# Transposing attention probabilities for tiles 4 to 23: one VectorE block transpose and eight SBUF-to-SBUF DMAs

## The chip, the core and the metric

The program runs on one core of a Trainium2 chip. The metric is the device time of one execution in microseconds (us), smaller is better. TensorE is called PE here, VectorE DVE, ScalarE ACT; SP is the queue from which this kernel issues all its DMAs. A "burst" is the run of small matmuls that PE does for one attention step.

## What is computed

A chunked local attention over 4 x 8 heads and 768 positions, followed by two feed-forward layers over all 3072 tokens:

```
scores = scale * q_chunk @ k_full.T          # chunk of 32, 16 left, 8 right, 8 memory keys
a = exp(scores - max); a = a / (sum(a) + 1e-9)
out_chunk = a @ v_full
x = out transposed to [3072, 512]
g = relu(x @ w_in) + alpha * min(x @ w_in, 0);  x = g @ w_out
h = x @ w2_in;  out = (h * tanh(softplus(h))) @ w2_out
```

## The kernel before

The 3072 tokens are worked in six blocks of 512 (four attention tiles of 128 tokens each, so 24 tiles T = 0 to 23). Layer 0 (first feed-forward) goes over the six blocks, then layer 1 does. In each block, `gemm1` (L697) makes 16 hidden groups j of 128 features, and `gemm2` (L761) adds them up; each is 12 matmuls of 128x512, since every fp32 product is made of three products of a high and a low half (`wh`,`wl` and `xh`,`xl` or `gh`,`gl`). The weights of layer 0 arrive in a raw form during block 0, and for each of the 32 weight tiles ACT does a scaling (L313) and a cast (L332) and DVE four instructions (L316, L319, L322, L335). The last of them, L335, writes the low half; `gemm2` of group j needs it by its third matmul.

Attention tiles 0 to 3 come first. Tiles 4 to 23 are woven into the layer-0 matmuls one block ahead: the burst "sv" does the scores of tile T+1 (L473) and right behind them the values of tile T (L540). Between the scores and the values of one tile lie: the maximum (DVE L488), eight exponentials (ACT L491), the normalisation (DVE L507) and the transposition of the probabilities `s` into `aT`, which puts keys on partitions. That last step is done in two ways:

- T < 7, `turn_pe`: PE transposes (16 small ones per tile, L583), then two copies from PSUM (L591, on ACT for tiles 4 to 6).
- T >= 7, `turn_dve`: eight DVE block transposes of 32 partitions x 256 (L609), each of which also moves its rows to other partitions.

For T >= 4 there is one `s` buffer and one `aT` buffer. Every step is entered in a `Plan` with an engine and an estimated duration; the planner (`run`, L107) works out an order for each engine, by what is due first among what it believes ready, and the program is issued in that order. Every engine, and SP's queue, then works strictly in its order. `block_steps` (L653 on) says which attention steps a block holds, `weave` spreads them evenly over the positions of the block. The engine's tile layer gives each DMA one of eight completion semaphores in turn, so a DMA waits until the eighth one before it has landed.

Of the kernel before, what the change touches and what calls it, by code (L numbers as in the profile page):

```python
# [68 lines left out]
class Plan:  # L69
# [13 lines left out]
    def add(self, eng, dur, fn, reads=(), writes=(), at=None, not_before=0.0):  # L83
        i = len(self.tasks)
        deps = set()
        for bufs, w in ((reads, False), (writes, True)):
            for b in bufs:
                b, part = (b[0], b[1:]) if isinstance(b, tuple) else (b, ())
                deps.update(t for t, p, tw in b.uses if (w or tw) and all(x == y for x, y in zip(p, part)))
                if w:  # L90
                    self.replaced.extend((i, old) for old in b.after)
                b.uses.append((i, part, w))
        deps.discard(i)
        if eng == "pe":
            at = self.now
            self.now += dur
        self.tasks.append((eng, dur, fn, deps, at, not_before))
        return i
# [76 lines left out]
def chunked_attention_moe_moe_kernel(  # L175
# [16 lines left out]
    nc = tc.nc  # L192
    P = 128
    B, UPB, W, H, D = vw.shape
# [5 lines left out]
    NP = H // 2  # L200
# [6 lines left out]
    CH = 32  # L207
    SW = 16 + CH + 8 + NM
# [1 line left out]
    TB = BN // P  # L210
    BLOCKS = [(t0, BN) for t0 in range(0, NT, BN)]
    NBA = len(BLOCKS)
    UPT = 7
    BOTH = ("act", "dve")
    WHOLE = (3,)
    T0 = BLOCKS[0][1] // P
# [20 lines left out]
    add = plan.add  # L237


    def a_(n):  # L240
        return 0.1 + 0.83e-3 * n

    def d_(n, fast=False):
        return 0.066 + n / (1920.0 if fast else 960.0)
# [4 lines left out]
    def copy_on(eng, out, in_):  # L249
        (nc.scalar.copy if eng == "act" else nc.vector.tensor_copy)(out, in_)  # L250
# [125 lines left out]
    def wide_of(b):  # L376
        return b.t.rearrange("p (g w) -> p g w", w=P)
# [20 lines left out]
    def att_bank(T, late):  # L398
        n_ps[0] += 1
        return bank((0, 1, 2, 4, 5, 6, 7)[n_ps[0] % 7] if T < T0 else late)  # L400
# [50 lines left out]
    def scores_of(T):  # L451

        t = T % TPB
        (kt, kview), (qt, qview) = kts[T], qs[T]
        bk = att_bank(T, 6)
        sb = s_bufs[T % 2 if T < T0 else 0]

        def s():
            return wide_of(sb)[:, :, CH : CH + SW]

        st = stats.next()
        ss[T] = sb

        def ps():
            return bk.t.rearrange("p (g c) -> p g c", c=SW)


        def go():
            for e in range(2):
                for p in range(NP):  # L470
                    for c in range(2):
                        k0 = e * (U + NM) + c * CH
                        nc.tensor.matmul(  # L473
                            ps()[c * 64 : (c + 1) * 64, e * NP + p, :],
                            qview()[:, p, e].rearrange("p h (x c) -> p (h x) c", c=2)[:, :, c],
                            kview()[:, p, k0 : k0 + SW],
                            start=True, stop=True,
                        )


        def clip():
            if t == 0:
                nc.vector.memset(ps()[0:64, 0:NP, 0:16], NEG)
            if t == TPB - 1:
                nc.vector.memset(ps()[64:128, NP:, SW - 8 :], NEG)

        def top():
            nc.vector.tensor_reduce(st.t[:, 0, :], ps(), AX.X, ALU.max, negate=True)  # L488

        def exps(g):  # L490
            nc.scalar.activation(  # L491
                s()[:, g, :], ps()[:, g, :], AF.Exp, bias=st.t[:, 0, g : g + 1], scale=0.125,
                accum_out=st.t[:, 1, g : g + 1],
            )


        def less():
            nc.vector.tensor_add(s(), ps(), st.t[:, 0, :].unsqueeze(2).broadcast_to([P, 2 * NP, SW]))

        def exp():  # L500
            nc.scalar.activation(s(), s(), AF.Exp, scale=0.125)

        def total():
            nc.vector.tensor_reduce(st.t[:, 1, :], s(), AX.X, ALU.add)

        def norm():
            nc.vector.tensor_mul(s(), s(), st.t[:, 2, :].unsqueeze(2).broadcast_to([P, 2 * NP, SW]))  # L507

        def rest():
            if t in (0, TPB - 1):  # L510
                add("dve", 0.15, clip, [], [bk])
            add("dve", d_(512), top, [bk], [(st, 0)])
            if T in WHOLE:
                add("dve", d_(512), less, [(st, 0), bk], [sb])
                add("act", a_(512), exp, [], [sb])
                add("dve", d_(512), total, [sb], [(st, 1)])
            else:
                add("dve", 0.12, lambda: nc.vector.tensor_scalar_mul(st.t[:, 0, :], st.t[:, 0, :], 0.125), [], [(st, 0)])
                for g in range(2 * NP):
                    add("act", 0.29, lambda g=g: exps(g), [(st, 0), bk], [(sb, g), (st, 1, g)])  # L520
            add("dve", 0.12, lambda: nc.vector.tensor_scalar_add(st.t[:, 2, :], st.t[:, 1, :], 1e-9), [(st, 1)], [(st, 2)])
            add("dve", 0.14, lambda: nc.vector.reciprocal(st.t[:, 2, :], st.t[:, 2, :]), [], [(st, 2)])
            add("dve", d_(512), norm, [(st, 2)], [sb])
            att_bufs.append(st)

        return go, [kt, qt], [bk], rest
# [41 lines left out]
    def turn_pe(T):  # L568
        sb = ss.pop(T)
        ab = a_bufs[T % 2 if T < T0 else 0]  # L570

        def aT():
            return ab.t[:W].rearrange("k (g h c q) -> k g h c q", g=2 * NP, h=2, c=2)

        aTs[T] = ab, aT
        for c in range(2):
            bk = att_bank(T, 6 + c)

            def turn(bk=bk, c=c):
                rows = slice(c * 64, (c + 1) * 64)  # L580
                k0 = (1 - c) * CH
                for g in range(2 * NP):
                    nc.tensor.transpose(  # L583
                        bk.t[0:W, g * 64 : (g + 1) * 64], wide_of(sb)[rows, g, k0 : k0 + W], ident[rows, rows]
                    )

            def back(eng, bk=bk, c=c):
                copy_on(eng, aT()[:, :, :, c, :], bk.t[0:W].rearrange("k (g h q) -> k g h q", g=2 * NP, h=2))

            add("pe", 0.6, turn, [sb] + behind(T), [bk])  # L590
            add(BOTH if T < T0 else "act", a_(512), back if T < T0 else partial(back, "act"), [bk], [(ab, c)])  # L591

    def turn_dve(T):

        sb, ab = ss.pop(T), a_bufs[0]

        def aT():
            return ab.t.rearrange("k (g h c q) -> k g h c q", g=2 * NP, h=2, c=2)

        aTs[T] = ab, aT  # L600
        for c in range(2):
            for h in range(2):
                for b in range(SW // CH):

                    def turn(c=c, h=h, b=b):
                        rows = slice((2 * c + h) * CH, (2 * c + h + 1) * CH)
                        keys = slice((c + b) * CH, (c + b + 1) * CH)
                        cols = slice(CH + b * CH, CH + (b + 1) * CH)
                        nc.vector.transpose(aT()[keys, :, h, c, :], wide_of(sb)[rows, :, cols])  # L609

                    add("dve", 0.34, turn, [sb], [(ab, (c, h, b))])

    def new_x(n):
        x = xring.next()
# [2 lines left out]
    def behind(T):  # L617

        return [last[0]] if T >= T0 and last else []
# [12 lines left out]
    def run_step(st):  # L632
        kind, T = st
        if kind == "t":
            turn_pe(T)
        elif kind == "v":
            burst(T, values_of(T))
        elif kind == "s":
            burst(T, scores_of(T))
        else:  # L640

            burst(T, scores_of(T), values_of(T - 1))
        if kind in ("s", "sv") and T0 - 1 <= T < NTT - 1:
            load_qk(T + 1)
        if kind in ("v", "sv"):
            done = T if kind == "v" else T - 1
            if T0 - 1 <= done < NTT - 1:
                load_v(done + 1)
        if kind in ("s", "sv") and T >= UPT:
            turn_dve(T)  # L650

    first = "s0 s1 t0 s2 t1 s3 v0 t2 v1 t3 v2 v3"
    block_steps = [[(st[0], int(st[1:])) for st in first.split()]]  # L653
    block_steps.append([("s", T0)])
    for T in range(T0, 2 * T0):
        block_steps[1] += [("t", T)] * (T < UPT) + [("sv", T + 1)]
    for blk in range(2, NBA):
        block_steps.append([("sv", T + 1) if T + 1 < NTT else ("v", T) for T in range(blk * TB, (blk + 1) * TB)])

# [172 lines left out]
    for st in block_steps[0]:  # L832
        run_step(st)
# [16 lines left out]
    for layer, blk, j in tiles:  # L850
# [13 lines left out]
        h = early[j] if (layer, blk) == (0, 0) and j < SPLIT else gemm1(layer, blk, j, xcur, n)  # L864
# [78 lines left out]
```

## Time and profile before

| what | value |
|---|---|
| time, median of 3 runs | 1127.35 us (1127.08 to 1128.28) |
| profiled execution: its own time / span | 1127.35 us / 1125.6 us |
| granted PE clock | 0.999 of full |
| busy PE / DVE / ACT | 1118.5 us (99%) / 828.1 us (74%) / 583.6 us (52%) |
| chain that ended last | PE 88%, DVE 8%, issue 1% |
| L609, DVE block transposes | 136 of 435 ns, 59.1 us |
| L583, PE transposes | 112 in all, 48 of them for tiles 4 to 6 |

The span begins with the first instruction of the profile and ends with the last; the time of the run has 1.75 us more around it. Matmul ends are modelled, so that PE is shown busy also where a matmul waited in its pipeline; the start times of successive matmuls tell the pace.

### The profile page before, as it was taken

Reading aid. Unit: us, or ns where it says so; the run is one execution under the profiler, and the core shown is the slowest. Engines: PE = TensorE matmul, PEld = TensorE weight load, DVE = VectorE, ACT = ScalarE, POOL = GpSimd, SP = SyncE. Lnnn points to the kernel's source line nnn. Section 1 sums busy time; section 2 is a strip of 40 time slices with the busy share of each in tenths; the row PEclk is TensorE's granted clock in tenths of the full one; section 3 lists DMA queues with packets and bytes.
Section 4 is the critical chain, followed back from the end, with each engine's and each line's share of the span. In section 5 each row is a group of like instructions: output and inputs, shape, how many; then the busy total and the mean of one; then the engine's idle time right before and its main releaser. Section 6 shows DMA issues by size and latency. Waiting matters only on the chain.

```text
span 1125.6 us, 16616 instructions
## 1 busy us (share of the span) xinstructions
PE 1118.5 (99%) x6320; PEld 921.7 (82%) x6320; DVE 828.1 (74%) x1452; ACT 583.6 (52%) x1270; POOL 6.8 (1%) x20
## 2 busy tenths in 40 slices
PE   9999999999999999999999999999999999999998
PEld 6888888888888888888888888888888888888886
DVE  7999954576667658645548778778878778777775
ACT  6887544454445545445446445446446445444543
POOL 2000000000000000000000000000000000000000
PEclk9999999999999999999999999999999999999999
DMA  9876312264454544434333002002001000100101
GB/s 279 240 224 186 90 44 53 70 190 120 120 158 121 155 137 134 124 103 132 102 94 103 1 1 75 1 1 75 1 1 63 13 1 20 38 1 1 38 1 38
DMA packets 71456, 94.28 MB, mean 84 GB/s; under 512 B 25296, under 2 KB 41680, under 8 KB 71376
## 3 DMA queue, kind: packets, MB, share of 16 engines
q1 hardware_dynamic: 71376, 93.22, 28.1%
q8 instruction: 49, 0.80, 0.3%
q14 instruction: 31, 0.25, 0.1%
HBM read 72.23 MB, written 20.97 MB: 83 GB/s over the span
## 4 chain that ended last, share of the span: by engine, by line
PE 88%; DVE 8%; issue 1%; ACT 0%; DVEq 0%
PE bank L761 43%; PE bank L697 42%; DVE wf L319 2%; DVE wf L322 1%; PE bank L473 1%; PE bank L540 1%; DVE gl L710 1%; DVE wf L316 1%; DVE rstrip L719 1%; DVE wo L335 1%; DVE aT L609 1%; DVE wi L335 0%; DVE s L507 0%; DVE st L488 0%; DVE xl L561 0%
## 5 line engine op out<-in xcount | busy, mean ns | idle before, releaser
L697 PE MATMUL bank<-xh,wi 128*128 128x512 f32 (+1 forms) x1552 | 506.2, 388 | 0.0
L697 PEld LDWEIGHTS bank<-xh,wi 128*128 128x128 f32 x1552 | 290.5, 188 | 60.1
L697 PE MATMUL bank<-xl,wi 128*128 128x512 f32 (+1 forms) x776 | 300.2, 387 | 0.0
L761 PE MATMUL bank<-gh,wo 128*128 128x512 f32 x768 | 254.0, 391 | 0.0
L761 PE MATMUL bank<-wo,gh 128*128 128x512 f32 x768 | 236.4, 389 | 0.0
L697 PEld LDWEIGHTS bank<-xl,wi 128*128 128x128 f32 x776 | 145.7, 188 | 29.2
L761 PEld LDWEIGHTS bank<-gh,wo 128*128 128x128 f32 x768 | 144.0, 188 | 30.9 <-DVE wo L335 0.4
L761 PEld LDWEIGHTS bank<-wo,gh 128*128 128x128 f32 x768 | 144.1, 188 | 29.9
L761 PE MATMUL bank<-gl,wo 128*128 128x512 f32 x384 | 149.5, 389 | 0.0
L761 PE MATMUL bank<-wo,gl 128*128 128x512 f32 x384 | 149.4, 389 | 0.0
L709 ACT CAST gh<-u 128x512 fp32r<-128x512 f32 x96 | 59.9, 623 | 155.9 <-PE bank L761 155.7
L719 DVE SCALAR_TENSOR_TENSOR rstrip<-rstrip,nalpha 128x512 f32<-128x512 f32 x96 | 71.9, 749 | 78.3 <-ACT rstrip L716 77.9
L709 ACT CAST gh<-rstrip 128x512 fp32r<-128x512 f32 x96 | 59.8, 623 | 108.5 <-PE bank L761 62.2
L710 DVE TENSOR_TENSOR gl<-rstrip,gh 128x512 fp32r<-128x512 f32 x96 | 66.1, 689 | 59.0 <-ACT gh L709 57.7
L715 ACT ACTIVATE rstrip<-bank 128x512 f32<-128x512 f32 x96 | 57.6, 600 | 97.4 <-PE bank L697 94.3
L728 ACT ACTIVATE u<-bank 128x512 f32<-128x512 f32 x96 | 57.4, 598 | 93.5 <-PE bank L697 92.7
L733 DVE SCALAR_TENSOR_TENSOR e<-n,rc 128x512 f32<-128x512 f32 x96 | 66.4, 691 | 48.5 <-ACT rc L732 48.5
L710 DVE TENSOR_TENSOR gl<-u,gh 128x512 fp32r<-128x512 f32 x96 | 66.3, 690 | 42.5 <-ACT gh L709 42.5
L761 PEld LDWEIGHTS bank<-wo,gl 128*128 128x128 f32 x384 | 72.1, 188 | 14.9
L761 PEld LDWEIGHTS bank<-gl,wo 128*128 128x128 f32 x384 | 72.1, 188 | 14.7
L731 ACT ACTIVATE e<-n,two 128x512 f32<-128x512 f32 x96 | 69.2, 720 | 4.4 <-DVE n L730 4.4
L734 DVE SCALAR_TENSOR_TENSOR rc<-e,rc 128x512 f32<-128x512 f32 x96 | 66.4, 691 | 3.2
(88 smaller groups left out, 1042.6 us busy)
## 6 DMA issues: line engine op xcount, KB each, us to landing
wi<-in_w_in_dram SPq DMA_DIRECT2D x16, 512.0 KB, 9.5
wo<-in_w_out_dram SPq DMA_DIRECT2D x16, 512.0 KB, 9.8
raw<-in_w_in_dram SPq DMA_DIRECT2D x16, 512.0 KB, 4.3
raw<-in_w_out_dram SPq DMA_DIRECT2D x16, 512.0 KB, 4.5
vw<-in_vw_dram SPq DMA_DIRECT2D x21, 384.0 KB, 3.9
kt<-in_kw_dram SPq DMA_DIRECT2D x21, 336.0 KB, 5.0
yd<-rstrip SPq DMA_DIRECT2D x24, 256.0 KB, 2.5
raw<-yd SPq DMA_DIRECT2D x24, 256.0 KB, 2.8
```

Source lines behind the costliest of these rows:

```text
L316: nc.vector.tensor_scalar(f.t, words()[1], 3, 0x7FFFFFFF, ALU.logical_shift_left, ALU.bitwise_and)
L319: nc.vector.scalar_tensor_tensor(f.t, words()[1], 0x80000000, f.t, ALU.bitwise_and, ALU.bitwise_or)
L697: nc.tensor.matmul(bk.t[:, lo:hi], a, b, start=kk == 0 and i == 0, stop=kk == KT - 1 and i == 2)
L709: add("act", a_(n), lambda: nc.scalar.copy(g.t[0], src.t[0]), [src], [(g, "h")])
L710: add("dve", d_(n), lambda: nc.vector.tensor_sub(g.t[1], src.t[0], g.t[0].bitcast(F32)), [src, (g, "h")], [(g, "l")])
L715: add("act", a_(n) - 0.05, lambda: nc.scalar.activation(m.t[0], h.t[:, :n], AF.Relu, scale=-1.0), [h], [m])
L719: lambda: nc.vector.scalar_tensor_tensor(r.t[0], m.t[0], nalpha[:, j : j + 1], r.t[0], ALU.mult, ALU.add),
L728: add("act", a_(BN) - 0.05, lambda: nc.scalar.activation(u.t, hs(), AF.Exp), [h], [u])
L731: add("act", a_(BN) + 0.09, lambda: nc.scalar.activation(e.t, n.t, AF.Ln, bias=two[:, 0:1]), [n], [e])
L733: add("dve", d_(BN), lambda: v.scalar_tensor_tensor(e.t, n.t, 2.0, r.t, ALU.add, ALU.mult), [n, r], [e])
L734: add("dve", d_(BN), lambda: v.scalar_tensor_tensor(r.t, e.t, 2.0, r.t, ALU.subtract, ALU.mult), [e], [r])
L761: nc.tensor.matmul(bk.t[:, :n], lt, rh, start=j == 0 and i == 0, stop=j == NJ - 1 and i == 2)
```

## The change

Tiles 4 to 23 are all transposed by a new function, `turn_dma`. The normalised probabilities of these tiles lie densely in the first 512 columns of `s`. One DVE instruction transposes all 32x32 blocks of all 128 partitions into columns 512 to 1023 of the same buffer, and eight DMAs on SP's queue, of 32 partitions x 256 columns (32 KB) each, carry the blocks to the partitions where `aT` wants them. `aT` is laid out anew (h, c, g, q in place of g, h, c, q), for the first four tiles too. The steps "t" of tiles 4 to 6 are gone, so block 0 holds five attention steps in place of eight and `weave` spaces them differently. `turn_pe` is left for tiles 0 to 3, with 0.85 in place of 0.6 as its estimate.

```
-    UPT = 7
...
-            return wide_of(sb)[:, :, CH : CH + SW]
+            return wide_of(sb)[:, :, CH : CH + SW] if T < T0 else sb.t[:, :512].rearrange("p (g w) -> p g w", w=SW)
...
-            return ab.t[:W].rearrange("k (g h c q) -> k g h c q", g=2 * NP, h=2, c=2)
+            return ab.t[:W].rearrange("k (h c g q) -> k g h c q", g=2 * NP, h=2, c=2)
...
-            add("pe", 0.6, turn, [sb] + behind(T), [bk])
+            add("pe", 0.85, turn, [sb] + behind(T), [bk])
...
-    def turn_dve(T):
+    def turn_dma(T):
...
+        def blocks():
+            nc.vector.transpose(
+                sb.t[:, 512:].rearrange("p (b g q) -> p b g q", b=SW // CH, q=CH),
+                sb.t[:, :512].rearrange("p (g b k) -> p b g k", b=SW // CH, k=CH),
+            )
+
+        add("dve", 0.85, blocks, [], [sb])
         for c in range(2):
-            for h in range(2):
-                for b in range(SW // CH):
-
-                    def turn(c=c, h=h, b=b):
-                        rows = slice((2 * c + h) * CH, (2 * c + h + 1) * CH)
-                        keys = slice((c + b) * CH, (c + b + 1) * CH)
-                        cols = slice(CH + b * CH, CH + (b + 1) * CH)
-                        nc.vector.transpose(aT()[keys, :, h, c, :], wide_of(sb)[rows, :, cols])
-
-                    add("dve", 0.34, turn, [sb], [(ab, (c, h, b))])
+            for b in range(SW // CH):
+
+                for h in range(2):
+
+                    def move(c=c, b=b, h=h):
+                        x0 = (2 * h + c) * 256
+                        nc.sync.dma_start(
+                            ab.t[(c + b) * CH : (c + b + 1) * CH, x0 : x0 + 256],
+                            sb.t[(2 * c + h) * CH : (2 * c + h + 1) * CH, 512 + b * 256 : 512 + (b + 1) * 256],
+                        )
+
+                    add("sp", 0.15, move, [sb], [(ab, (c, h, b))])
...
-        if kind in ("s", "sv") and T >= UPT:
-            turn_dve(T)
+        if kind in ("s", "sv") and T >= T0:
+            turn_dma(T)
...
-        block_steps[1] += [("t", T)] * (T < UPT) + [("sv", T + 1)]
+        block_steps[1] += [("sv", T + 1)]
```

What this does to the order of the instructions is shown at three places, all in block 0.

DVE, around the transposition of tile 8, the last one of block 0, before (`wo` and `wf` are weights of layer 0 and their scratch tile, `st` the statistics of the softmax):

```order
L322 SCALAR_TENSOR_TENSOR wf_1553<-wo_1328,wf_1553 128x512
L319 SCALAR_TENSOR_TENSOR wf_1568<-wo_1394,wf_1568 128x512
L521 TENSOR_SCALAR st_1536<-st_1536 128x8
L322 SCALAR_TENSOR_TENSOR wf_1568<-wo_1394,wf_1568 128x512
L522 RECIPROCAL st_1536<-st_1536 128x8
L335 TENSOR_TENSOR wo_1582<-wf_1553,wo_1582 128x512
L507 TENSOR_TENSOR s<-s,st_1536 128x8x64
L719 SCALAR_TENSOR_TENSOR rstrip<-rstrip,nalpha 128x512
L609 STREAM_TRANSPOSE aT<-s 32x8x32 x8
```

and the same place of the changed kernel (lines there are one lower up to about L650, and ten higher from L707 on):

```order
L520 TENSOR_SCALAR st_1490<-st_1490 128x8
L321 SCALAR_TENSOR_TENSOR wf_1523<-wo_1337,wf_1523 128x512
L521 RECIPROCAL st_1490<-st_1490 128x8
L720 TENSOR_TENSOR gl<-rstrip,gh 128x512
L506 TENSOR_TENSOR s<-s,st_1490 128x512
L334 TENSOR_TENSOR wo_1548<-wf_1523,wo_1548 128x512
L603 STREAM_TRANSPOSE s<-s 128x512
L321 SCALAR_TENSOR_TENSOR wf_1520<-wo_1386,wf_1520 128x512
L729 SCALAR_TENSOR_TENSOR rstrip<-rstrip,nalpha 128x512
```

Eight instructions have become one, and the third instruction on the last weight tile (L322, now L321) and the last L719 stand behind the transposition in place of ahead of it.

SP, the end of block 0's loads, before:

```order
L299 DMA wo_1328<-in_w_out_dram 128x1024
L447 DMA vw_1343<-in_vw_dram 96x2x512
L413 DMA kt_1359<-in_kw_dram 128x672
L433 DMA qbd_101<-in_q_dram 64x8x64 x2
L299 DMA wo_1394<-in_w_out_dram 128x1024
```

and now:

```order
L298 DMA wo_1337<-in_w_out_dram 128x1024
L616 DMA aT<-s 32x256 x8
L432 DMA qbd_101<-in_q_dram 64x8x64 x2
L298 DMA wo_1386<-in_w_out_dram 128x1024
L446 DMA vw_1434<-in_vw_dram 96x2x512
L412 DMA kt_1445<-in_kw_dram 128x672
L432 DMA qbd_90<-in_q_dram 64x8x64 x2
L616 DMA aT<-s 32x256 x8
```

The two groups of eight are the moves of tiles 7 and 8; the load of the last weight tile of layer 0 (`wo15`) stands behind those of tile 7.

PE, where tile 4 was transposed before:

```order
L697 MATMUL bank_692<-xl_359,wi_662 128x512
L697 MATMUL bank_692<-xh_358,wi_662 128x512
L583 MATMUL bank_720<-ident,s 96x64 x8
L583 MATMUL bank_732<-ident,s 96x64 x8
L761 MATMUL bank_604<-gh,wo_696 128x512
```

and the burst that now uses tile 4's `aT`:

```order
L707 MATMUL bank_811<-xh_357,wi_802 128x512
L472 MATMUL bank_819<-kt_667,qbd_101 64x64 x16
L539 MATMUL bank_836<-aT,vw_635 64x64 x16
L707 MATMUL bank_811<-xh_357,wi_802 128x512
L707 MATMUL bank_811<-xl_358,wi_802 128x512
```

The rows of L583 are gone for tiles 4 to 6. The values of tiles 4 to 8 now stand behind 123, 180, 246, 300 and 384 large matmuls of block 0 and its successor, before behind 120, 192, 264, 309 and 384; from tile 8 on the places are the same as before.

## Rows read from the trace of the kernel before

**Rows 1.** Windows view (us): busy time (count) per engine, clock, DMA share, GB/s

```profile
110.00:120.00 10.00, 10.00 (x50) 7.98 (x47) 10.00 (x19) 5.74 (x12) 0.00 (x0) 1.00 0.43 100
```

**Rows 2.** Chain of waits in order of time: start, length, what

```profile
130.20 2.96 PE bank L697 x12
...
1107.67 13.61 PE bank L761 x60
```

**Rows 3.** PE timeline around tile 4's transposition: start, length, line

```profile
46.74 0.39 PE L697 MATMUL bank<-xh,wi 128*128 128x512 f32 x1
47.05 0.92 PE L583 MATMUL bank<-ident,s 64*96 64x64 f32 x16
...
48.24 0.40 PE L761 MATMUL bank<-gl,wo 128*128 128x512 f32 x1
```

**Rows 4.** PE timeline: weight tile wo13, and the bursts of tiles 8 and 9

```profile
119.69 0.73 PE L761 MATMUL bank<-gh,wo 128*128 128x512 f32 x2
...
127.64 1.18 PE L473 MATMUL bank<-kt,qbd 128*64 128x64 f32 x32
128.65 1.55 PE L540 MATMUL bank<-aT,vw 96*64 96x64 f32 x32
130.13 0.50 PE L697 MATMUL bank<-xh,wi 128*128 128x512 f32 x1
...
147.72 1.10 PE L540 MATMUL bank<-aT,vw 96*64 96x64 f32 x32
148.75 0.50 PE L697 MATMUL bank<-xh,wi 128*128 128x512 f32 x1
```

**Rows 5.** DVE timeline of the end of block 0

```profile
105.11 3.59 DVE L609 STREAM_TRANSPOSE aT<-s 32x256 f32<-32x256 f32 x8
108.73 0.43 DVE L316 TENSOR_SCALAR wf<-wo 128x512 uint32<-128x512 uint32 x1
...
118.95 0.68 DVE L335 TENSOR_TENSOR wo<-wf,wo 128x512 fp32r<-128x512 f32 x1
119.55 0.16 DVE L518 TENSOR_SCALAR st<-st 128x8 f32<-128x8 f32 x1
...
121.21 0.42 DVE L316 TENSOR_SCALAR wf<-wo 128x512 uint32<-128x512 uint32 x1
...
124.75 0.74 DVE L719 SCALAR_TENSOR_TENSOR rstrip<-rstrip,nalpha 128x512 f32<-128x512 f32 x1
125.41 3.59 DVE L609 STREAM_TRANSPOSE aT<-s 32x256 f32<-32x256 f32 x8
```

**Rows 6.** Groups by line: count, busy us, mean ns, idle before

```profile
L609 DVE STREAM_TRANSPOSE aT<-s 32x256 f32<-32x256 f32 x136 | 59.1, 435 | 2.6
L322 DVE SCALAR_TENSOR_TENSOR wf<-wi,wf 128x512 uint32<-128x512 uint32 x16 | 10.9, 682 | 0.1
L521 DVE TENSOR_SCALAR st<-st 128x8 f32<-128x8 f32 x24 | 4.0, 168 | 7.0 <-ACT s L491 6.8
```

**Rows 7.** SP timeline: start and length of the issue of DMAs

```profile
148.86 0.33 SPq L447 DMA_DIRECT2D vw<-in_vw_dram  x1
149.25 0.44 SPq L413 DMA_DIRECT2D kt<-in_kw_dram  x1
```

**Rows 8.** Time from issue to landing: stores L784; DMA view, loads of q

```profile
DMA to landing us min/median/max: 2.0/2.1/2.6
...
qbd<-in_q_dram SPq DMA_DIRECT2D x40, 128.0 KB, 5.5
```

**Rows 9.** Line L540 from 146 to 150 us, and PE's weight loads there

```profile
L540 PEldq EVENT_SEMAPHORE  x1: 51/51/51, 147.1 to 147.1; - x1
...
147.66 1.02 PEld L540 LDWEIGHTS bank<-aT,vw 96*64 96x64 f32 x32
```

**Rows 10.** DVE timeline, tile 9: normalisation and last transposes

```profile
136.46 0.69 DVE L507 TENSOR_TENSOR s<-s,st 128x512 f32<-128x512 f32 x1
...
139.71 2.26 DVE L609 STREAM_TRANSPOSE aT<-s 32x256 f32<-32x256 f32 x5
```

More of the change, by code (lines that the diff above doesn't have):

```diff
@@ L588, in back @@
                 copy_on(eng, aT()[:, :, :, c, :], bk.t[0:W].rearrange("k (g h q) -> k g h q", g=2 * NP, h=2))
-            add("pe", 0.6, turn, [sb] + behind(T), [bk])
+            add("pe", 0.85, turn, [sb] + behind(T), [bk])
             add(BOTH if T < T0 else "act", a_(512), back if T < T0 else partial(back, "act"), [bk], [(ab, c)])
-    def turn_dve(T):
+    def turn_dma(T):
         sb, ab = ss.pop(T), a_bufs[0]
         def aT():
-            return ab.t.rearrange("k (g h c q) -> k g h c q", g=2 * NP, h=2, c=2)
+            return ab.t[:W].rearrange("k (h c g q) -> k g h c q", g=2 * NP, h=2, c=2)
         aTs[T] = ab, aT
-        for c in range(2):
-            for h in range(2):
-                for b in range(SW // CH):
-                    def turn(c=c, h=h, b=b):
-                        rows = slice((2 * c + h) * CH, (2 * c + h + 1) * CH)
-                        keys = slice((c + b) * CH, (c + b + 1) * CH)
-                        cols = slice(CH + b * CH, CH + (b + 1) * CH)
-                        nc.vector.transpose(aT()[keys, :, h, c, :], wide_of(sb)[rows, :, cols])
-                    add("dve", 0.34, turn, [sb], [(ab, (c, h, b))])
+        def blocks():
[4 more added lines that the diff above has]
+        add("dve", 0.85, blocks, [], [sb])
+        for c in range(2):
+            for b in range(SW // CH):
[7 more added lines that the diff above has]
+                    add("sp", 0.15, move, [sb], [(ab, (c, h, b))])
     def new_x(n):
```

## The prediction

> **What bounds the kernel now.** I began with the chain of waits. From 130.20 us to its last piece, which ends at 1121.28, its pieces are PE work in groups of twelve matmuls per 2.72 us [rows 2], 0.227 us apiece. The bursts in it are PE work too, and nothing waits. So whatever comes after the values burst of tile 8 is a fixed amount of PE work: the end of the run moves by what the end of that burst moves, and the change can win or lose only before 130 us, or by bringing a wait into a stretch that has none.
>
> The windows come next. In block 0, DVE is busy all the time: 10.00 of 10 us from 110 to 120 [rows 1]. It must take 32 weight tiles apart while PE already uses them. PE keeps its pace of 0.227 us there as well, so the two engines run side by side, and I looked for the places where PE meets DVE. There are two. The third matmul of gemm2 on weight tile wo13 starts at 119.69 [rows 4], right after the instruction that writes that tile's low half (118.95, 0.68 long) [rows 5]. And the values of tile 8 start at 128.65 and last 1.55 [rows 4], while the eight transposes that make their input run from 125.41 for 3.59 us [rows 5]. An undisturbed values burst takes 148.75 - 147.72 = 1.03 us to the next matmul [rows 4], so this one, which ends at 130.13, lost 0.45.
>
> **What PE saves.** Tiles 4 to 6 no longer use PE. A transposition costs it 48.24 - 46.74 - 2 x 0.227 = 1.05 us [rows 3]; three make 3.1 us. That would be the gain if PE alone decided. It does not: PE then comes to wo13 3.1 us earlier and finds DVE still at work.
>
> **What DVE saves up to wo13.** It loses the eight transposes of tile 7, 108.73 - 105.11 = 3.62 us [rows 5]. It gets one transposition of 512 elements for each of tiles 4 to 7. Counting the changed DVE order up to wo13's low half, there is besides one 128x512 copy less (in the first tiles, now on ACT; 0.60, the distance of such instructions, 119.55 - 118.95 [rows 5]) and one instruction of 8 columns more (0.08, my estimate, half its own 0.168 [rows 6]).
>
> The new instruction appears nowhere in the trace. Below, it is bounded by 0.60, what any 128x512 instruction occupies; above by two of today's at 3.62 / 8 = 0.45, so 0.90. I take 0.70: an instruction on 512 columns lasts 0.682 and one on 8 columns 0.168 [rows 6], about 1.0 ns per column, and 256 columns more on top of the 0.435 of today's transpose [rows 6] give 0.70.
>
> So DVE reaches wo13 earlier by 3.62 + 0.60 - 4 x 0.70 - 0.08 = 1.34 us. PE's third matmul on it goes from 119.69 to 118.35. Between it and the scores and values of tile 8 PE has the same work in both orders (34 large matmuls), so the values would start at 128.65 - 1.34 = 127.31.
>
> **When tile 8's probabilities arrive.** Ahead of tile 8's transposition DVE has, besides the eight transposes and the copy, one L322 (0.60) and one L719 (125.41 - 124.75 = 0.66 [rows 5]) less, which the new order puts behind it, and the four new ones more: it starts at 125.41 - 3.62 - 0.60 - 0.60 - 0.66 + 2.80 = 122.73 and ends at 123.43. The moves come in place of the last 2.9 us of DVE work. SP has nothing left in front of them then but loads that wait for tile 7's values, long done. SP issues DMAs 149.25 - 148.86 = 0.39 apart [rows 7]; the first at about 123.48, the eighth at 126.21. Landing is unknown for a 32 KB move inside SBUF; nearest are the 256 KB stores, 2.0 to 2.6, median 2.1 [rows 8]. With 2.1 the last block is there at 128.3, later than PE at 127.31, so PE waits 1.0 us and the burst ends at 128.3 + 0.05 + 1.03 = 129.4, against 130.13. Gain 0.75 us.
>
> The Trainium skill speaks against splitting the move. "DMA: Bandwidth & Descriptors", Rules for kernel authors, says of transfers to disjoint partition halves "Don't bother — they serialize", and advises one transfer over all partitions. Taken at its hardest, the eight landings would follow one another; that is rival 5. In the rows the loads vw and kt are issued 0.39 us apart, far less than any landing takes, so the issue at least does not wait; whether 32 KB moves land side by side, no row shows.
>
> **What is hidden.** Tiles 4 to 7 get their values in the same way, 5.6 us after the start of their transposition (0.70 + 0.05 + 7 x 0.39 + 2.1). If a burst waits for that, PE only loses what it would have waited for wo13, up to 3.1 - 1.34 = 1.8 us in all. From tile 9 on the slack is larger. Tile 9's normalisation starts at 136.46, its transposes end at 139.71 + 2.26 = 141.97, and its values start at 147.72 [rows 10, 4]; with the change, 136.46 + 0.69 + 0.05 + 5.6 = 142.8, still 4.9 ahead. Without that cover each later burst would cost what it is late. The 3 us of DVE and the 6 ACT copies that are saved are worth nothing by themselves. The loads behind the moves: wo15's stands behind tile 7's moves, whose transposition starts at about 101.4 (105.11 less 3.7 of DVE work), so it is issued about 106 and DVE's first instruction on it ran at 121.21 [rows 5]. The other weight loads behind moves have as much. The new layouts and the new spacing of block 0's steps change no count of matmuls, so nothing. New waits on PE: a values burst now waits for up to eight DMA semaphores ahead of its first two matmuls. Such a wait takes 51 ns on PE's queue, and it ran at 147.1 for a weight load at 147.66 [rows 9], so 0.56 us ahead; I count it as hidden.
>
> **Sum.** Against the profiled execution's own 1127.35 us, which is also the median: 1127.35 - 0.75 = 1126.6 us. Bounds of this case: with 0.60 per transposition, issues every 0.33 (the vw issue's own length [rows 7]) and a landing of 2.0, PE is ready at 126.91, the last block lands at 127.3 and the burst ends at 128.4: 1125.6. With 0.90, no gain from the copy, 0.44 per issue and 2.6, the transposition ends at 125.03, the last block lands at 130.8, the burst ends at 131.8: 1129.0.
>
> **Rivals.** A change of 0.2%, 2.25 us, is about what a measurement of this kernel can tell from none.
>
> 1. *The forecast*, 1125.6 to 1129.0, at 1126.6. For it: DVE's full windows and the two meetings. 0.66.
> 2. *PE alone decides block 0.* All of 3.1 us and the 0.45 of tile 8's wait come out: 1123.8. It needs DVE 1.8 us faster by wo13 and the moves done before 125.5. For it: DVE's order is rebuilt and the meetings are few. Against it: no free DVE time before 130. 0.12.
> 3. *The semaphore waits show.* At most four more per burst in 20 bursts at 51 ns, 4.1 us: 1130.7; slower from 0.15 us a burst on. For it: a burst of 32 ns matmuls drains PE's queue. Against it: the 0.56 us of lead. 0.09. The Trainium skill, "TensorE: Matmul & The Clock Gate", its table of specifications, gives PE a queue of 64 entries, which would hide them too; what a wait in the middle of a burst does, no row shows.
> 4. *Tile 8's moves land like the loads of q*, 5.5 us [rows 8]: burst done at 132.7, 1130.0; slower than before as soon as a landing takes 2.9, by more than 0.2% from 5.1. For it: block 0's traffic. Against it: the loads are out by 107, except kt, vw and q of tile 9. 0.09.
> 5. *The moves land one after another*, 8 x 2.1: 140.3 for tile 8, burst done 141.3, at least 1138.5. 0.04, since the rows show overlapped issue.
>
> **How the numbers follow.** The time is that of rival 1. Faster by over 0.2% (below 1125.1) is rival 2: 0.12. Slower (above 1129.6) are 4, 5 and half of 3: 0.18. The rest, 0.70, is no change. The range goes from 1124.4, which takes in half of rival 2, to 1130.0, which takes in rival 4 and half of rival 3; it leaves out about 0.15.
>
> **What would show it.** New transposition 0.60 to 0.90 us; PE waiting before wo13 and other weight tiles between 60 and 120 us; wo13's third matmul near 118.35; tile 8's transposition at 122.7; its moves 0.39 apart, landing in 2.0 to 2.6; its values ending near 129.4; no PE wait after that. I am wrong if DVE idles in block 0, if a later burst waits for a move, or if the pace within the bursts falls.

## The result

The changed kernel takes 1141.26 us (median of 6 runs, 1137.81 to 1145.79) against 1127.79 for the kernel before (6 runs beside it): ratio 1.0119, 95% interval 1.0102 to 1.0137. It is slower by 13.5 us. The forecast of 1126.6, and its range up to 1130.0, were wrong.

Where the time went is read from the profiled execution of the changed kernel, whose own time is 1140.33 us (span 1138.5, granted clock 0.999). Its chain of waits and its PE timeline answer to [rows 2, 4]:

```profile
137.19 1.18 PE L472 MATMUL bank<-kt,qbd 128*64 128x64 f32 x32
140.20 0.30 PE L539 MATMUL bank<-aT,vw 96*64 96x64 f32 x2 [1.82 <-DMA aT<-s]
140.83 1.12 PE L539 MATMUL bank<-aT,vw 96*64 96x64 f32 x30 [0.33 <-DMA aT<-s]
141.88 0.50 PE L707 MATMUL bank<-xh,wi 128*128 128x512 f32 x1
...
158.46 1.19 PE L472 MATMUL bank<-kt,qbd 128*64 128x64 f32 x32
159.48 1.10 PE L539 MATMUL bank<-aT,vw 96*64 96x64 f32 x32
160.51 0.50 PE L707 MATMUL bank<-xh,wi 128*128 128x512 f32 x1
```

```profile
331.91 4.97 DMA raw<-in_w_in_dram
...
1121.22 13.61 PE bank L771 x60
```

Tile 8's values end at 141.88, against 130.13 before: 11.75 us of the 13.55 by which the last piece moved (1121.22 against 1107.67) were lost in block 0. Another 1.8 came near 332 us, where the chain runs through a load of the second layer's weights. Tile 9's values (159.48, 1.03 us to the next matmul) and those behind it wait for nothing.

In block 0 the windows, which answer to [rows 1], no longer show a saturated DVE, and PE is no longer full (columns as there: PE, PE's weight loads, DVE, ACT, POOL, clock, DMA share, GB/s):

```profile
80.00:90.00 10.00, 8.53 (x37) 6.46 (x35) 8.23 (x17) 6.52 (x24) 0.00 (x0) 1.00 0.99 297
90.00:100.00 10.00, 9.18 (x87) 7.44 (x88) 9.24 (x18) 5.14 (x10) 0.00 (x0) 0.83 0.40 103
...
110.00:120.00 10.00, 8.71 (x92) 7.11 (x91) 7.98 (x15) 4.81 (x9) 0.00 (x0) 1.00 0.60 151
```

The chain of waits says what they wait for. At the last weight tile, wo15, it runs along SP's queue: moves of tile 7 (L616), the loads of q behind them (L432), the landing of wo15, and ACT's scaling of it (L312):

```profile
112.84 0.59 SPq L616
...
113.47 0.59 SPq L432
...
114.11 0.63 SPq L432
...
114.78 6.64 DMA wo<-in_w_out_dram
...
121.44 0.03 ACT wo L312
```

The chain has four such `DMA wo` pieces, of 8.16, 7.28, 7.66 and 6.64 us, after the moves of tiles 4, 5, 6 and 7. Two of them end a wait of ACT: the 7.28 (issued at 76.18) one of 3.49 us, the 6.64 one of 4.90 us. The other two the chain joins to DVE's L603, before which DVE did not stand still, so these two prove no wait. The waits view counts what ACT lost to late weight loads between 30 and 145 us (us, times, longest), 16.7 us in all:

```profile
ACT wo L312 <- DMA wo<-in_w_out_dram: 13.6, 5, 4.9
...
ACT wi L312 <- DMA wi<-in_w_in_dram: 3.1, 3, 1.2
```

SP's timeline of the changed kernel shows the groups of eight moves (x8) and the loads right behind them:

```profile
51.56 5.02 SPq L616 DMA_DIRECT2D aT<-s  x8
56.62 0.58 SPq L298 DMA_DIRECT2D wo<-in_w_out_dram  x1
...
108.42 5.00 SPq L616 DMA_DIRECT2D aT<-s  x8
113.47 1.27 SPq L432 DMA_DIRECT2D qbd<-in_q_dram  x2
114.78 0.62 SPq L298 DMA_DIRECT2D wo<-in_w_out_dram  x1
```

The next rows are from the ACT, DVE and PE timelines at that place. They show how the late load gets to PE:

```profile
121.44 0.67 ACT L312 ACTIVATE wo<-wo 128x512 f32<-128x512 f32 x1 [4.90 <-DMA wo<-in_w_out_dram]
122.01 0.60 ACT L331 CAST wo<-wf 128x512 fp32r<-128x512 f32 x1
...
122.64 0.69 DVE L334 TENSOR_TENSOR wo<-wf,wo 128x512 fp32r<-128x512 f32 x1 [4.66 <-ACT wo L331]
...
122.66 0.50 PE L771 MATMUL bank<-gh,wo 128*128 128x512 f32 x1 [1.09 <-ACT wo L331]
```

wo15 lands at 121.42. ACT, which works in order, stands 4.90 us before its scaling of it (L312). Queued behind is L331, which casts the high half of another weight tile, wo12, loaded long before. DVE's L334 needs that cast and stands 4.66 us, and PE's next matmul, the first on wo12, starts at 122.66. In the kernel before, SP issued wo15 at 100.20 and ACT scaled it at 106.71 without waiting (SP's and ACT's timelines of before):

```profile
100.20 0.61 SPq L299 DMA_DIRECT2D wo<-in_w_out_dram  x1
```

```profile
106.71 0.65 ACT L313 ACTIVATE wo<-wo 128x512 f32<-128x512 f32 x1
```

Its wo6, issued at 42.21, was scaled at 58.93. Now wo6 goes out at 56.62 and ACT waits 3.33 us for it.

### The profile page after: what moved, and what is told of

Its sections match the earlier page's. It is cut to its first block, busy times and chain, and to the rows that moved or that the text cites. A ratio compares the mean times of both kernels' runs of the same rounds, so it can differ in the third digit from the quotient of the medians.

```text
span 1138.5 us, 16691 instructions
## 1 busy us (share of the span) xinstructions
PE 1121.3 (98%) x6270; PEld 921.5 (81%) x6270; DVE 780.2 (69%) x1335; ACT 580.1 (51%) x1265; POOL 6.6 (1%) x20
## 4 chain that ended last, share of the span: by engine, by line
PE 90%; DMA 3%; DVE 2%; SPq 2%; ACT 1%; issue 1%; DVEq 0%; ACTq 0%
PE bank L707 43%; PE bank L771 43%; DMA wo<-in_w_out_dram 3%; PE bank L472 2%; PE bank L539 2%; SPq L616 1%; PE bank L833 1%; DMA raw<-in_w_in_dram 0%; DVE wf L318 0%; ACT s L490 0%; DVE wf L321 0%; SPq L432 0%; DVE s L603 0%; DVE gl L720 0%; DVE wf L315 0%
## 5 line engine op out<-in xcount | busy, mean ns | idle before, releaser
L707 PE MATMUL bank<-xh,wi 128*128 128x512 f32 (+1 forms) x1552 | 507.4, 388 | 0.6 <-DVE wi L334 0.6
L707 PEld LDWEIGHTS bank<-xh,wi 128*128 128x128 f32 x1552 | 290.5, 188 | 61.2 <-DVE wi L334 1.1
L707 PE MATMUL bank<-xl,wi 128*128 128x512 f32 (+1 forms) x776 | 300.3, 387 | 0.0
L771 PE MATMUL bank<-gh,wo 128*128 128x512 f32 x768 | 255.5, 393 | 3.0 <-ACT wo L331 1.6
L771 PE MATMUL bank<-wo,gh 128*128 128x512 f32 x768 | 236.4, 389 | 0.0
L771 PEld LDWEIGHTS bank<-gh,wo 128*128 128x128 f32 x768 | 144.5, 188 | 36.2 <-ACT wo L331 2.5
L707 PEld LDWEIGHTS bank<-xl,wi 128*128 128x128 f32 x776 | 146.0, 188 | 29.4
L771 PEld LDWEIGHTS bank<-wo,gh 128*128 128x128 f32 x768 | 144.1, 188 | 29.9
L771 PE MATMUL bank<-gl,wo 128*128 128x512 f32 x384 | 150.3, 391 | 2.7 <-DVE gl L720 2.7
L771 PE MATMUL bank<-wo,gl 128*128 128x512 f32 x384 | 149.4, 389 | 0.0
L719 ACT CAST gh<-u 128x512 fp32r<-128x512 f32 x96 | 59.9, 623 | 155.9 <-PE bank L771 155.7
L719 ACT CAST gh<-rstrip 128x512 fp32r<-128x512 f32 x96 | 59.9, 624 | 62.2 <-PE bank L771 39.7
L771 PEld LDWEIGHTS bank<-gl,wo 128*128 128x128 f32 x384 | 72.4, 188 | 18.3 <-DVE gl L720 3.7
L771 PEld LDWEIGHTS bank<-wo,gl 128*128 128x128 f32 x384 | 72.1, 188 | 15.0
```

What stands on the lines that cost most here:

```text
L707: nc.tensor.matmul(bk.t[:, lo:hi], a, b, start=kk == 0 and i == 0, stop=kk == KT - 1 and i == 2)
L719: add("act", a_(n), lambda: nc.scalar.copy(g.t[0], src.t[0]), [src], [(g, "h")])
L771: nc.tensor.matmul(bk.t[:, :n], lt, rh, start=j == 0 and i == 0, stop=j == NJ - 1 and i == 2)
```

## The experiments

Theory Q: the loads stand behind the moves in SP's in-order queue, come late, and ACT holds back DVE and PE. Rival M: the moves themselves are late for the values (the bursts of tiles 5, 7 and 8 wait 1.47, 1.29 and 2.15 us). Rival O: the planner's new order on DVE and ACT costs the time. Rival S: the additional semaphore waits of the bursts. Times below are medians, beside the kernel before on the same chip.

**Moves off SP's queue.**

```
-                        nc.sync.dma_start(
+                        nc.gpsimd.dma_start(
                             ab.t[(c + b) * CH : (c + b + 1) * CH, x0 : x0 + 256],
```

> The changed kernel with its moves issued by GpSimd; the order of the work on PE, VectorE and ScalarE is the same row for row, and SP's queue keeps its loads in the same order. Theory Q (weight loads stand behind the moves in SP's queue): ScalarE no longer waits 13.6 us for wo loads before 145 us, VectorE is back at 9.7 or more of 10 us up to 100 us, tile 8's values end near 130, and the time is 1125 to 1130. Rival M (the moves themselves come too late for the values, 5.0 us from first to eighth issue): the waits of values bursts for moves stay at 3.9 us or grow, and block 0 still ends near 140: 1137 or more. Rival O (the new order on VectorE and ScalarE costs the time): nothing changes but a few us, 1136 or more.

Measured: 1135.76 against 1127.64, ratio 1.0068 (1.0053 to 1.0083). Half of theory Q's forecast came true: between 30 and 145 us one wait of 0.80 us for a weight load is left on ACT. Yet only about 5 of the 13.5 us came back. PE's timeline shows M in their place:

```profile
72.73 1.19 PE L472 MATMUL bank<-kt,qbd 128*64 128x64 f32 x32
77.51 2.17 PE L539 MATMUL bank<-aT,vw 96*64 96x64 f32 x32 [3.59 <-DMA aT<-s]
79.61 0.80 PE L771 MATMUL bank<-gh,wo 128*128 128x512 f32 x1
```

The line's own view, L616 from 66 to 80 us, gives the reason: issues 0.5 us apart, a little quicker than SP's 0.63, but landings about three to four times the 1.8 us of the changed kernel.

```profile
L616 POOL DMA_DIRECT2D aT<-s x8: 496/497/498, 68.9 to 72.4; - x8
...
DMA to landing us min/median/max: 5.1/6.2/7.1
```

The 512 KB loads are now in flight at the same time: from 68 to 72 us the DMA engines' busy share is 1.06 and more. In the changed kernel the moves held the loads back (a share of 0.21 to 0.45 from 70 to 74 us), and landed fast.

**The queue alone, in the kernel before.** Spare DMAs that wait for the normalisation of tiles 4 to 8, in the place in SP's order that a move would have by the planner's rule, eight or one for each tile:

```
+    def spare_move(sb, k):
+        p = slice(k % 4 * CH, (k % 4 + 1) * CH)
+        nc.sync.dma_start(spare[p, :], sb.t[p, 288:352])
...
+            if T0 <= T <= 8:
+                plan.probes += [(i, partial(spare_move, sb, k)) for k in range(8)]
```

> The kernel before with its own transpositions, and besides for each of tiles 4 to 8 eight spare DMAs of 32x64 elements on SP, which wait for the tile's normalisation and are read by nobody; the rows of PE, VectorE and ScalarE stay in the order of before. Theory Q: loads behind them come late, ScalarE waits for them, VectorE idles: 1132 to 1140. Rival M: nobody waits for these moves, so 1127 to 1128.5. Rival O: 1127 to 1128.5.

> As the kernel with spare DMAs, but one for each of tiles 4 to 8 instead of eight. In the changed kernel SP stood waiting for VectorE for 46.6 us before 145 us and took 5.0 us to issue each group of eight. If the wait at the head of the queue is what delays the loads, one DMA does nearly the same as eight: 1131 or more. If the issue of eight is what delays them, this kernel is near the one before: 1127 to 1129.

Measured: eight, 1136.61, ratio 1.0072 (1.0056 to 1.0088); one, 1127.14, ratio 0.9993 (0.9984 to 1.0003). With eight, ACT waits 12.3 us for weight loads; with one, for none. SP's own waits are nearly equal (with eight, then with one):

```profile
SPq L458 <- DVE s L516: 36.9, 5, 12.2
```

```profile
SPq L458 <- DVE s L516: 35.0, 5, 12.5
```

35 us of standing at the head of the queue cost nothing; five groups of 5.0 to 6.4 us of issues cost 9 us, in the order of before, with PE's and DVE's old transpositions and no one who reads the result. That is Q, with the issue and not the wait as its cost: such a loss needs neither M nor O. What M adds in the changed kernel these two runs cannot say. Nor is all of the 35 us additional: in the kernel before, SP already stood 59.7 us up to 145 us ahead of the loads of `vw`, with one spare DMA only 32.8 us.

**Nobody waits for the moves.** On SP, and all on GpSimd:

```
+                        if T <= 8:
+                            nc.sync.dma_start(spare[p, :], sb.t[p, 512 + b * 256 : 576 + b * 256])
+                            return
```

> The changed kernel, its rows in the same order on PE, VectorE and ScalarE, but the eight moves of tiles 4 to 8 write 32x64 elements to a spare tile, and the values of these tiles read what stood in the turned tile before (so the output of tiles 4 to 8 is not attention). What is left of the moves is their place in SP's queue. Theory Q (loads behind 5.0 us of issues): most of the loss stays, 1134 to 1140, with ScalarE still waiting for wo loads. Theory M (the values wait for moves): nothing waits for them any more, so 1124 to 1128.

> All moves on GpSimd, those of tiles 4 to 8 with 32x64 elements to a spare tile, and the values of these tiles read what stood in the turned tile before (so the output of tiles 4 to 8 is not attention). SP's queue holds only loads and nobody waits for moves in block 0. If the 8.1 us that the moves cost on GpSimd are values that wait for moves which land in 5.1 to 7.1 us among the loads, nothing is left of them and PE's saving of 3.1 us shows: 1123 to 1126. If the new order on VectorE and ScalarE costs something of its own, 1128 or more.

Measured: on SP 1142.27, ratio 1.0116 (1.0088 to 1.0144); on GpSimd 1125.22, ratio 0.9981 (0.9972 to 0.999). On SP a loss as large is there although no burst waits for a move. ACT's waits in that run (us, times, longest):

```profile
ACT wo L312 <- DMA wo<-in_w_out_dram: 14.1, 5, 6.4
...
ACT wi L312 <- DMA wi<-in_w_in_dram: 8.8, 3, 4.6
```

They are 22.9 us, 6.2 more than in the changed kernel. So this run is not simply the changed kernel without M: two of a tile's spare moves write the same rows, the later one waits for the earlier to land, and SP's groups last 5.9 to 7.5 us in place of 5.0. The run shows that the loss needs no waiting burst; how much M adds to the changed kernel's loss stays open. On GpSimd, M was all of the loss, as far as these runs tell (the spare moves carry a quarter of the bytes). With neither, the order that O blames is 2 us faster than before. O falls for the changed kernel.

**How many issues.** Four or six of the eight moves on SP, the rest on GpSimd:

```
-                        nc.sync.dma_start(
+                        (nc.gpsimd if h else nc.sync).dma_start(
```

> The changed kernel with four of the eight moves issued by GpSimd and four by SP. SP then issues moves for 2.5 us per tile instead of 5.0, and the eight are out in about 2.5 us. With the moves wholly on GpSimd the loss was 8.1 us, wholly on SP 13.5. If both the loads behind the moves and the values behind the moves cost by time of issue, both parts fall to about half: 1131 to 1135. If what decides is that moves share the DMA engines with loads in flight, as their landings of 5.1 to 7.1 us on GpSimd suggest, it stays near the run on GpSimd: 1134 to 1138.

> The changed kernel with six moves of a tile on SP (3.7 us) and two on GpSimd, every engine's other rows in the order of the changed kernel. Four on SP gave 1126.9 and eight 1141.3. If the loads lose what SP issues beyond a slack of about 2.5 us, five times over, six lie between: 1131 to 1136. If the loss comes in one step, with all eight (the completion semaphores all taken by moves, or the last move being what values wait for), six are near four: 1126 to 1129.

Measured: four 1126.93, ratio 0.9986 (0.9972 to 1.0); six 1132.38, ratio 1.0042 (1.0026 to 1.0057). With eight it was 1141.26. The first was better than either expectation. Put in a row with the run that has none on SP and no waiting burst (1125.22): the first four issues, 2.5 us a tile, cost 1.7 us in all; the next two, 1.25 us a tile or 6.25 over five tiles, cost 5.5; the last two, as much again, 8.9. An estimate from these four medians: SP has a slack of some 2.5 us a tile, and beyond it the kernel pays about what SP issues. The last step seems to hold some of M too, since the bursts' waits for moves grow from 1.5 us with six to 3.9 with eight. The loss does not come in one step with the eighth move, as it would if it lay in all completion semaphores being taken by moves; and in the changed kernel SP goes on from the last move to the next load within 0.04 us, without a wait for a landing. With four, no burst waits, and the moves on GpSimd land fast too. SP's own four still hold the loads back: the DMA engines' share is 0.28 from 68 to 70 us. L616, 66 to 80 us:

```profile
L616 SPq DMA_DIRECT2D aT<-s x4: 567/589/604, 67.8 to 69.7; - x4
L616 POOL DMA_DIRECT2D aT<-s x4: 498/498/498, 68.3 to 69.8; - x4
...
DMA to landing us min/median/max: 1.7/1.8/2.3
```

**The planner's estimate.** `add("sp", 0.15, move, ...)` became 0.62 on SP alone, and 0.31 with two queues:

> The changed kernel, with the planner told 0.62 us instead of 0.15 for each move, the distance at which SP issued them. The planner then puts SP's loads and VectorE's transpositions elsewhere. If the loss is one of order (loads that could stand ahead of moves, transpositions that could run earlier), the time falls to 1128 to 1136. If SP's 5.0 us of issues per tile are the cost wherever they stand, it stays at 1137 or more.

> Moves on two queues as in the run before, and the planner told 0.31 us a move (half of 0.62, since two queues issue at once) instead of 0.15. In the run on two queues PE still lost 1.74 us between 80 and 90 us to a load of wo that was issued behind moves. If a planner that knows the price puts such loads ahead, block 0 keeps PE's saving of 3.1 us: 1123.5 to 1126. If the other order costs as much elsewhere, 1126 to 1129.

Measured: SP alone 1135.26, ratio 1.0058 (1.0037 to 1.008); two queues 1125.05, ratio 0.998 (0.9971 to 0.9989). The true price wins back 6 us of the loss on SP. The 7.5 us that are left there are not Q as it was read above: ACT waits 2.5 us for weight loads, no burst waits for a move, but PE waits for casts of weights (L331), once 3.6 us, ahead of 114.27, while DVE works almost without a gap from 104 to 115.9:

```profile
PE bank L771 <- ACT wo L331: 3.8, 2, 3.6
```

This suggests that the order which the planner then makes has a price of its own; it was not taken apart. With two queues the true price makes a kernel that beats both the changed kernel and the one before: 2.2 us faster than before. Its waits in block 0 are nearly gone, and tile 8's values end 1.37 us earlier than before (PE timeline, then the chain's last piece):

```profile
127.73 1.10 PE L539 MATMUL bank<-aT,vw 96*64 96x64 f32 x32
128.76 0.50 PE L707 MATMUL bank<-xh,wi 128*128 128x512 f32 x1
```

```profile
1105.53 13.61 PE bank L771 x60
```

The last piece comes 2.14 us earlier than 1107.67. Most of the other 0.8 us were gained in block 0 as well: by the trace, PE has done three large matmuls more when this burst begins (411 in place of 408), 0.68 us of work.

**Only from tile 9 on.** Tiles 4 to 8 turned as before, by PE and by the eight transposes (`if kind in ("s", "sv") and T >= 9: turn_dma(T)`). In this kernel those turns read the old spacing of `s` while the probabilities were written in the dense one, so tiles 4 to 8 get other values.

> The transposition in blocks and the moves for tiles 9 and later only; tiles 4 to 6 are turned by PE and 7 and 8 by VectorE's eight transposes, with the new layout of the turned tile. If the loss lies with the loads of block 0, tile 8's values end at 130 to 131 and only the wait near 332 us for a load of the second layer's weights is left, about 1.8 us: 1127 to 1130. Rival S (every values burst pays for its additional semaphore waits): 1130 or more, with bursts after 150 us longer than 1.03 us.

Measured: 1126.97, ratio 0.9991 (0.9982 to 1.0001). Nothing is lost in or behind block 0. S falls, and the expected 1.8 us at 332 us did not appear either, although tiles 9 and later use all eight moves on SP. In the changed kernel SP issues moves there from 311.84 for 5.01 us and a load of the second layer's weights right behind them, at 316.96; ACT waits 6.33 us for that load and 4.68 us for the next, of 331.91. The order alone does not bring it about: in the run on SP in which nobody waits, which has the changed kernel's order, PE is busy 10.00 of 10 us from 340 to 350, where the changed kernel has 8.76. The cause of the 1.8 us stays open.

**Two that told other things than intended.**

```
-        block_steps[1] += [("sv", T + 1)]
+        block_steps[1] += [("s", T + 1), ("v", T)]
```

> Moves on GpSimd, and in block 0 the scores of a tile and the values of the tile before no longer stand in one burst: the values come some 30 large matmuls (about 6.8 us) later. If all that was left of the loss on GpSimd was values waiting for their moves (7.0 us of waits and what these delayed), the waits go and the time is 1124 to 1129; each more burst costs PE about 0.3 us. If the order on VectorE and ScalarE is what costs the rest, 1133 or more.

Measured: 1142.25, ratio 1.0123 (1.01 to 1.0147). The edit put a tile's values behind the *next* tile's turning in the program, so they read the next tile's probabilities and waited for its moves as well. It says nothing on the question; the run on GpSimd in which nobody waits answered it.

```
-                nc.sync.dma_start(
+                (nc.gpsimd if layer == 0 else nc.sync).dma_start(
                     t.rearrange("p (k f) w -> p k (f w)", k=KT),
```

> The changed kernel with all eight moves on SP as before, and the loads of the first layer's weights issued by GpSimd instead, so that they stand behind no move; the rows of PE, VectorE and ScalarE stay in their order. If the place of these loads behind the moves is the whole loss, and moves land in 1.8 us as they did on SP, only the short waits of values for moves that were seen in the changed kernel (about 5 us together, against 3.1 saved) are left: 1126 to 1130. If the loads, no longer held back, fill the DMA engines so that the moves land in 5 to 7 us as they did on GpSimd, the values wait: 1132 to 1137.

Measured: 1142.44, ratio 1.0135 (1.0112 to 1.0158), worse than either expectation; the profiled execution, 1137.37, is the fastest of the four. ACT waits 0.7 us for weight loads after 20 us, once. But little but their own landings holds the loads back now: GpSimd has issued them all by 58.5 us, the DMA engines are full, tile 5's scores wait for q, and tile 4's moves take up to 7.7 us. The windows, and L616 from 50 to 60 us:

```profile
50.00:60.00 10.00, 7.85 (x45) 6.05 (x45) 10.00 (x19) 6.90 (x13) 3.68 (x6) 1.00 1.06 347
60.00:70.00 10.00, 6.03 (x69) 5.12 (x65) 3.71 (x9) 1.63 (x3) 0.00 (x0) 0.66 1.07 327
```

```profile
L616 SPq DMA_DIRECT2D aT<-s x8: 507/586/590, 52.3 to 59.5; - x8
DMA to landing us min/median/max: 5.6/7.6/7.7
```

So the order in SP's queue was not only an obstacle. It also rationed the DMA engines.

## Why the prediction was wrong, step by step

- **The step that failed** is under "What is hidden": "wo15's stands behind tile 7's moves ... so it is issued about 106 and DVE's first instruction on it ran at 121.21 ... The other weight loads behind moves have as much." It costed the loads behind the moves at nothing. Its error is in the cover, not only in the delay. The first engine that needs the tile is ACT, which scaled it at 106.71 in the trace of before, 6.5 us after the issue at 100.20; 121.21 is the second engine's row. From that the step took away no landing, which was 6.64 us for wo15 in the changed kernel. With its own 106 the load would have been ready near 112.6, 6 us late for ACT's place for it. In the run it went out at 114.78, since block 0 was late by then, and ACT waited 4.90 us. And one tile stood for all: ACT waits eight times, 16.7 us.
- **The mis-sized term**: moves 0.39 us apart. They are 0.63 apart (eight in 5.02). The 0.39 came from the loads vw and kt; the q loads of 64 partitions, in the same trace of before 1.21 us for two, were the nearer row. By itself this moves tile 8's last landing by 7 x 0.24 = 1.7 us. It hurts by lengthening what the loads stand behind, from 3.1 to 5.0 us a tile, further beyond the slack of some 2.5.
- **Right**: the transposition takes 0.71 us (0.70 predicted; 20 of them, 708 ns). The median landing of moves on SP is 1.8 (2.1). Of PE's saving of 3.1 us about 2.2 showed in the best version. Where neither loads nor bursts wait (moves on GpSimd, read by nobody), tile 8's values start at 126.93, near the sum's 127.31. From tile 9 on no burst waits for a move: values at 159.48 start right behind the scores. The semaphore waits stay hidden: the burst of tile 9 keeps its 1.03 us. "No PE wait after that" was off by the 1.8 us near 332.
- **"DVE decides"** did not hold: DVE idles in block 0, where it waits for ACT, and tile 8's transposition starts at 133.60 instead of 122.73.
- **The rivals**: five were listed, and the one that happened was not among them, a load behind a waiting and slowly issuing move. Rival 4 (moves that land like loads) is real, but only where the loads are not held back: 5.1 to 7.7 us. Rival 5 falls: moves started 0.63 apart land in 1.8 us in the median, 3.5 at most. The sentence "Don't bother — they serialize" (the Trainium skill, "DMA: Bandwidth & Descriptors", Rules for kernel authors) is not borne out for moves of 32 KB that are issued this slowly; the measurement decides.
- The same page, Issuing engines are not separate DMA queues, says that a second issuing engine saves only the time of initiating a DMA, "usually small relative to the DMA itself". That the issuing is what is saved agrees with the runs. Small it is not here: 0.63 us of issue beside 1.8 of landing, and 14.3 us of the kernel's time between eight issues on SP and four.

## What to carry to other kernels

Price a DMA that is added to an in-order queue by what stands behind it: its issue time times its count, against the slack of the next load at the *first* engine that touches the load, with the landing taken off. Here the wait at the head of the queue was free and the issue of eight was not, so vary the count before blaming the wait. And moving traffic to a free queue also takes the pacing away: split it, and tell a scheduler the measured price.

## What was not expected of the hardware

The issue of a small SBUF to SBUF move takes 0.59 us on SP, much the same in both sizes that were run: 32x256 elements (589 ns median) and 32x64 (0.55 to 0.59 alone), while a load of 96x2x512 takes 0.33 at its shortest. On GpSimd it takes 0.50. A move lands in 1.8 us on quiet DMA engines and in up to 7.7 among 512 KB loads.

PE's granted clock can fall after PE stood still. In the changed kernel PE stood 0.55 and 1.74 us between 88 and 91 us, and from 92 to 94 us the clock was 0.50, the lower of its two levels (1.2 of 2.4 GHz). It stayed at 1.00 after the waits at 75 us (1.47 us in all) and at 140 us (2.15). In the run with moves on GpSimd, after 3.59 us of waiting, it was 0.50 up to 82 us: the matmuls of L771 start 0.60 apart at 79.61 and about 0.42 apart at 81.49, near twice the usual 0.227. So a wait in block 0 can cost more than its own length.
